# A planner that prefers matmuls whose operands have lain ready for a while

## The chip, the cores and the metric

The kernel runs on one core of one Trainium2 chip. The metric is the device time of one execution in microseconds (us); lower is better. Before the change the median of three runs is 1119.1 us (1116.96, 1119.1 and 1125.9).

## The reference

Attention over 4 batches, 8 heads, 768 positions and a head size of 64, in which a query sees only the keys whose 6 hash bits equal its own; its output goes through a two-layer feed-forward block with a squared ReLU.

```python
q_bits = (np.einsum('bhsd,dk->bhsk', q, proj) > 0).astype(np.int64)
k_bits = (np.einsum('bhsd,dk->bhsk', k, proj) > 0).astype(np.int64)
mask = q_bucket[:, :, :, None] == k_bucket[:, :, None, :]      # buckets: the 6 bits as a number
scores = np.where(mask, 0.125 * np.matmul(q, k.transpose(0, 1, 3, 2)), -1000000000.0)
attn = np.exp(scores - np.max(scores, axis=-1, keepdims=True))
attn = attn / (np.sum(attn, axis=-1, keepdims=True) + 1e-09)
x = np.matmul(attn, v)                       # then to [3072 tokens, 512]
r = np.maximum(x @ w_in, 0.0)                # w_in 512 x 2048
return (s * (r * r) + b) @ w_out             # w_out 2048 x 512
```

## The kernel before, in words

**Slots.** The attention is cut into 96 slots: one head of one batch and one chunk of 256 queries each. In batch 0 the 8 heads are visited once for chunk 0 and once for chunks 1 and 2; in batches 1 to 3 each head is visited once, for its three chunks. On TensorE (PE) a slot is a chain with steps of VectorE (DVE) between:

- scores: six matmuls with 256 columns (L527; L525 for the first eight slots) into banks 0 to 2 of PSUM; DVE takes the maximum (L532)
- two transposes of that maximum into bank 4 (L536); DVE reduces them (L538)
- one small transpose of the result into bank 4 (L540); DVE makes a row of it (L546)
- six matmuls that add this row and the low parts (L557); ScalarE (ACT) takes the exponential (L562)

These steps of PE are the slot's chain. What follows is not in it: the exponentials are split in two by ACT (L579) and GpSimd (POOL, L580) and go through the values matmuls (L586, L587) into bank 3; the sums of a row (L614) go to bank 4; and the operands of the head after next are prepared with transposes (L386), hash matmuls (L411 to L413) and a mean (L488), all in the other half of bank 4, which ACT and DVE read (L388, L389, L416).

**Feed-forward work.** The output of two heads goes to DRAM (`xd`), and when all 8 heads of a chunk are there it is loaded again (`xc`, four DMAs of 256 KB on SP's queue, L649). A chunk then takes 192 matmuls with 256 columns (L662, bank 5) and 96 with 512 columns (L679, banks 6 and 7). There are twelve chunks. The two tiles of `xc` hold one chunk, so the next chunk's load starts when the last L662 of the one before is done. Weights are made in batch 0 from decoded words.

**What sets the order.** Every step is recorded with an engine, a cost, the names that it reads and writes, and a priority `pr` (low goes first): chain and scores near 10 x the slot's number, the rest of the attention a little behind, feed-forward work at 1e5 and above. `Plan.order` plays the engines forward by these costs: a step's `ready` is the planned end of what it depends on plus a hop (`HOP`, 0.2 us behind PE, 0.06 behind DVE, ACT and POOL, 1.8 behind SP). When an engine is free, it takes among the steps that are ready the one with the lowest `(pr, index)`. So on PE the feed-forward matmuls fill whatever the attention leaves. The steps are then issued in the order of their planned starts, each engine works through its own list strictly in that order, and semaphores see to the real dependencies. The plan names the halves of bank 4 as two things, `("b", 4, 0)` for chain and sums and `("b", 4, 1)` for preparation.

```python
    def pe(cost, fn, r, w, pr):
        plan.add(PE, cost, fn, r, w, pr)
```

Of the kernel before, what the change touches and what calls it, by code (L numbers as in the profile page):

```python
# [31 lines left out]
class Plan:  # L32
# [3 lines left out]
    def __init__(self):  # L36
        self.steps = []
        self.writer = {}
        self.readers = {}

    def add(self, eng, cost, fn, r=(), w=(), pr=0.0, lag=0.0):
        i = len(self.steps)
# [15 lines left out]
    def order(self):  # L58
        n = len(self.steps)
        left = [len(s[5]) for s in self.steps]  # L60
        users = [[] for _ in range(n)]
        for i, s in enumerate(self.steps):
            for d in s[5]:
                users[d].append(i)
        ready = [0.0] * n
        free = {}
        moved = 0.0
        open_ = {}
        for i in range(n):
            if not left[i]:  # L70
                open_.setdefault(self.steps[i][0], []).append(i)
        out = []
        while len(out) < n:
            best = None
            for e, lst in open_.items():
                if lst:
                    t = max(free.get(e, 0.0), min(ready[i] for i in lst))
                    if best is None or t < best[0]:
                        best = (t, e)
            t, e = best  # L80
            rank = lambda i: (self.steps[i][3], i)
            i = min((i for i in open_[e] if ready[i] <= t), key=rank)
            i = min((j for j in open_[e] if ready[j] <= t + LOOK.get(e, 0.0) * self.steps[i][1] and rank(j) <= rank(i)), key=rank)
            open_[e].remove(i)
            eng, cost, fn, pr, lag, deps = self.steps[i]
            start = max(free.get(e, 0.0), ready[i])
            free[e] = start + cost
            end = start + cost + HOP[e]
            if e == SP:
                moved = max(moved, start + cost) + lag  # L90
                end += moved - start - cost
            else:
                end += lag
            out.append((start, i))
            for u in users[i]:
                ready[u] = max(ready[u], end - (SAME[e] if self.steps[u][0] == e else 0.0))
                left[u] -= 1
                if not left[u]:
                    open_.setdefault(self.steps[u][0], []).append(u)
        self.length = max(free.values())  # L100
        self.start = {i: t for t, i in out}
        return [i for _, i in sorted(out)]
# [2 lines left out]

HOP = {None: 0.0, PE: 0.2, DVE: 0.06, ACT: 0.06, POOL: 0.06, SP: 1.8}
SAME = {None: 0.0, PE: 0.2, DVE: 0.06, ACT: 0.06, POOL: 0.06, SP: 0.0}
LOOK = {DVE: 0.5, ACT: 0.0, POOL: 0.0}


@with_exitstack
def lsh_attention_moe(ctx: ExitStack, tc, q, k, v, proj, w_in, w_out, s, b, out):
    nc = tc.nc
# [32 lines left out]

        plan.add(SP, 0.7, lambda: nc.sync.dma_start(f32(dst()), f32(src())), r, w, pr, size / 2.6e5)

    def pe(cost, fn, r, w, pr):
        plan.add(PE, cost, fn, r, w, pr)  # L150

    def dve(n, fn, r, w, pr, ns=None):
        plan.add(DVE, ((n + 64) / 960.0 if ns is None else ns), fn, r, w, pr)
# [7 lines left out]
    def mmc(n, c):  # L161
        return c * (n / 2325.0 + 0.0095)
# [348 lines left out]
    def scores(i, pr):  # L511
# [7 lines left out]
        for p in range(NP_):  # L519
            def lead(p=p):  # L520
                for m in range(2):
                    o, kt = bank[:, pb[p], m * CH:(m + 1) * CH], slice((2 * p + m) * P, (2 * p + m + 1) * P)
                    if exact:
                        n = P if i < WARM else HR
                        nc.tensor.matmul(o, EK[h][0:n, kt], EQ[h][0:n, cs], start=m == 0, stop=m == 1, skip_group_check=True)  # L525
                        continue
                    nc.tensor.matmul(o, ks[0:HR + TPC, 0, kt], aq[0:HR + TPC, cs], start=m == 0, stop=m == 1, skip_group_check=True)  # L527
            pe(mmc(CH, 8 if exact else 2), lead, AK(x) + KK(x) if exact else AK(x, g=(c,))  + KK(x, (0, 2, 4)), [("b", pb[p])], pr)
        t, tk, nm, nk = MX, "mx", nmt[:, i % 4], ("nm", i % 4)

        sc = bank[:, b0:b0 + NP_].rearrange("p b (m n) -> p n b m", n=CH)
# [2 lines left out]
        def across():  # L534
            for j in range(TPC):
                nc.tensor.transpose(out=bank[:, 4, j * P:(j + 1) * P], in_=t[:, j * P:(j + 1) * P], identity=ident)  # L536
        pe(0.23, across, [tk], [("b", 4, 0)], pr)
        dve(CH, lambda: nc.vector.tensor_reduce(nm, bank[:, 4, 0:CH].rearrange("p (j n) -> p j n", j=TPC), AX.X, ALU.max, negate=True), [("b", 4, 0)], [nk], pr, 0.41)  # L538

        pe(0.115, lambda: nc.tensor.transpose(out=bank[0:TPC, 4, 0:P], in_=nm, identity=ident), [nk], [("b", 4, 0)], pr)  # L540
        mr, mk = (zhl[0:TPC, y], ("mrow", y)) if exact else (bq[0:TPC, cs], ("mr", x, c))

        def rows():
# [6 lines left out]
        for p in range(NP_):  # L550
            def rest(p=p):
                for m in range(2):
# [2 lines left out]
                        nc.tensor.matmul(o, oner[0:TPC], mr, start=False, stop=m == 1, skip_group_check=True)  # L555
                        continue
                    nc.tensor.matmul(o, ks[:, 1, kt], bq[:, cs], start=False, stop=m == 1, skip_group_check=True)  # L557
            pe(mmc(CH, 2), rest, [mk, tk] + ([] if exact else BK(x, g=(c,)) + KK(x, (1, 3))), [("b", pb[p])], pr)
        ES = [(npiece[0] + p) % (NE + 2 * NHL) for p in range(NP_)] if plain(i) else list(range(NP_))
        npiece[0] += NP_  # L560
        for p, z in enumerate(ES):
# [236 lines left out]
```

## Time and profile before

| what | value |
|---|---|
| median of three runs | 1119.1 us |
| the profiled execution's own time | 1128.45 us |
| its span | 1126.7 us |
| PE busy | 1063.8 us (94%), 6862 matmuls |
| weight loads of PE busy | 918.7 us (82%) |
| ACT, POOL, DVE busy | 700.5, 683.4, 655.9 us |
| mean granted clock of PE | 0.973 |

The span is what the profile sees of the execution; 1.75 us lie around it. PE is the engine with the most work by far. A matmul's end in this profile is modelled, so that idle time of PE shows only the part of a wait that reaches beyond it; the starts of consecutive matmuls and the idle time of the weight loads tell the rest.

### The profile page before, as it was taken

Reading aid. Unit: us, or ns where it says so; the run is one execution under the profiler, and the core shown is the slowest. Engines: PE = TensorE matmul, PEld = TensorE weight load, DVE = VectorE, ACT = ScalarE, POOL = GpSimd, SP = SyncE. Lnnn points to the kernel's source line nnn. Section 1 sums busy time; section 2 is a strip of 40 time slices with the busy share of each in tenths; the row PEclk is TensorE's granted clock in tenths of the full one; section 3 lists DMA queues with packets and bytes.
Section 4 is the critical chain, followed back from the end, with each engine's and each line's share of the span. In section 5 each row is a group of like instructions: output and inputs, shape, how many; then the busy total and the mean of one; then the engine's idle time right before and its main releaser. Section 6 shows DMA issues by size and latency. Waiting matters only on the chain.

```text
span 1126.7 us, 18822 instructions
## 1 busy us (share of the span) xinstructions
PE 1063.8 (94%) x6862; PEld 918.7 (82%) x6862; DVE 655.9 (58%) x807; ACT 700.5 (62%) x1377; POOL 683.4 (61%) x617
## 2 busy tenths in 40 slices
PE   8998788789999999999999999998999999999998
PEld 5665567678888888888888888887888998898987
DVE  5575767566676777677777677776776751000000
ACT  5566767566776777677766777776766773333332
POOL 4355788667576767676767676766676873222221
PEclk8888989899999999999999999999999999999999
DMA  7644444332422332332333243323232202101010
GB/s 164 177 134 133 121 139 138 91 83 72 117 72 62 109 93 74 87 99 57 81 99 89 59 111 77 80 62 118 55 79 82 64 11 75 38 19 56 1 57 19
DMA packets 99404, 94.49 MB, mean 84 GB/s; under 512 B 68528, under 2 KB 72112, under 8 KB 99312
## 3 DMA queue, kind: packets, MB, share of 16 engines
q1 hardware_dynamic: 94112, 76.24, 25.8%
q10 hardware_dynamic: 5200, 17.05, 5.0%
q8 instruction: 54, 0.88, 0.3%
q14 instruction: 38, 0.31, 0.1%
HBM read 49.81 MB, written 18.87 MB: 61 GB/s over the span
## 4 chain that ended last, share of the span: by engine, by line
PE 67%; DVE 4%; ACT 3%; issue 3%; POOL 3%; DMA 2%; SPq 0%; ACTq 0%; DVEq 0%; POOLq 0%
PE bank L662 21%; PE bank L679 20%; PE bank L557 5%; PE bank L527 4%; PE bank L587 4%; PE bank L586 4%; PE bank L536 2%; PE bank L614 2%; PE bank L386 2%; POOL hl L580 2%; DMA xd<-xsb 1%; PE bank L411 1%; PE bank L540 1%; ACT aq L388 1%; DVE nmt L538 1%
## 5 line engine op out<-in xcount | busy, mean ns | idle before, releaser
L580 POOL TENSOR_TENSOR hl<-et,hl 128x512 fp32r<-128x512 f32 x216 | 278.4, 1318 | 149.3 <-ACT hl L579 142.7
L662 PE MATMUL bank<-xc,w 128*128 128x256 f32 x2304 | 338.4, 286 | 6.8 <-DMA xc<-xd 5.7
L662 PEld LDWEIGHTS bank<-xc,w 128*128 128x128 f32 x2304 | 305.4, 189 | 17.1 <-DMA xc<-xd 3.4
L679 PE MATMUL bank<-w,ghb 128*128 128x512 f32 x768 | 257.7, 397 | 0.0
L670 POOL TENSOR_TENSOR glb<-rb,ghb 128x512 fp32r<-128x512 f32 x96 | 124.5, 1297 | 144.6 <-ACT ghb L669 134.1
L532 DVE TENSOR_REDUCE mx<-bank 128x256 f32<-128x1536 f32 x96 | 168.0, 1750 | 49.2 <-PE bank L527 30.2
L679 PE MATMUL bank<-w,glb 128*128 128x512 f32 x384 | 153.7, 403 | 0.0
L679 PEld LDWEIGHTS bank<-w,ghb 128*128 128x128 f32 x768 | 136.7, 188 | 16.9 <-issue 0.3
L608 DVE TENSOR_REDUCE zb<-et 128x256 f32<-128x1536 f32 x72 | 126.0, 1750 | 41.2 <-ACT et L562 38.6
L562 ACT ACTIVATE et<-bank 128x512 f32<-128x512 f32 x240 | 130.7, 621 | 26.1 <-PE bank L557 18.5
L667 ACT ACTIVATE rb<-bank 128x512 f32<-128x512 f32 x96 | 57.2, 595 | 142.6 <-PE bank L662 139.4
L579 ACT CAST hl<-et 128x512 fp32r<-128x512 f32 x216 | 128.6, 661 | 0.8
L527 PE MATMUL bank<-aq,ks 78*128 78x256 f32 x528 | 122.6, 316 | 2.1 <-ACT ex L562 1.5
L586 PE MATMUL bank<-hl,vs 128*128 128x256 f32 x432 | 119.7, 295 | 0.0
L587 PE MATMUL bank<-hl,vs 128*128 128x256 f32 x432 | 114.7, 286 | 1.1 <-POOL hl L580 0.8
L527 PEld LDWEIGHTS bank<-aq,ks 78*128 78x128 f32 x528 | 91.2, 197 | 14.9 <-ACT ex L562 3.7
L687 DVE SCALAR_TENSOR_TENSOR osb<-bank,misc,bcs 128x512 f32<-128x512 f32 x22 | 16.2, 745 | 140.8 <-PE bank L679 140.7
L618 ACT ACTIVATE xpb<-bank,vmn 64x256 f32<-64x256 f32 x96 | 45.0, 469 | 80.9 <-PE bank L587 80.0
L557 PE MATMUL bank<-bq,ks 128*128 128x256 f32 x528 | 82.3, 292 | 11.5 <-DVE bq L546 11.5
L587 PEld LDWEIGHTS bank<-hl,vs 128*128 128x128 f32 x432 | 81.9, 189 | 7.7 <-POOL hl L580 4.5
L624 DVE RECIPROCAL zpb<-zpb 128x256 f32<-128x256 f32 x48 | 83.7, 1744 | 3.2 <-ACT zpb L616 2.9
L557 PEld LDWEIGHTS bank<-bq,ks 128*128 128x128 f32 x528 | 70.5, 192 | 17.3 <-DVE bq L546 8.8
(111 smaller groups left out, 1676.6 us busy)
## 6 DMA issues: line engine op xcount, KB each, us to landing
xd<-xsb SPq DMA_DIRECT2D x48, 256.0 KB
xc<-xd SPq DMA_DIRECT2D x48, 256.0 KB
raw<-in_moe_w_in_dram ACTq DMA_DIRECT2D x16, 512.0 KB
raw<-in_moe_w_out_dram ACTq DMA_DIRECT2D x16, 512.0 KB
nat<-in_q_dram SPq DMA_DIRECT2D x32, 192.0 KB
nat<-in_k_dram SPq DMA_DIRECT2D x32, 192.0 KB
bq<-aq SPq DMA_DIRECT2D x32, 192.0 KB
out_dram<-osb SPq DMA_DIRECT2D x22, 256.0 KB
```

The lines of the kernel that those rows point to most:

```text
L527: nc.tensor.matmul(o, ks[0:HR + TPC, 0, kt], aq[0:HR + TPC, cs], start=m == 0, stop=m == 1, skip_group_check=True)
L532: dve(S * TPC, lambda: nc.vector.tensor_reduce(t, sc, AX.XY, ALU.max), [("b", b) for b in pb], [tk], pr, 1.75)
L557: nc.tensor.matmul(o, ks[:, 1, kt], bq[:, cs], start=False, stop=m == 1, skip_group_check=True)
L562: act(512, lambda p=p, z=z: nc.scalar.activation(et(z) if plain(i) else pairs(z), bank[:, pb[p]] if plain(i) else bank[:, pb[p]].rearrange ...
L579: act(512, lambda z=z, y=y: nc.scalar.copy(HL[2 * y].rearrange("p (m n) -> p m n", n=CH), pairs(z)), [("e", z)], [("hl", 2 * y)], pr)
L580: pool(512, lambda z=z, y=y: nc.gpsimd.tensor_tensor(HL[2 * y + 1].rearrange("p (m n) -> p m n", n=CH), pairs(z), f32(HL[2 * y]).rearrange ...
L586: nc.tensor.matmul(av, VS[w % 2][:, kt], HL[2 * y][:, ms], start=(kt == 0), stop=False)
L587: nc.tensor.matmul(av, VS[w % 2][:, kt], HL[2 * y + 1][:, ms], start=False, stop=(kt == NT - 1))
L608: dve(S * TPC, lambda: nc.vector.tensor_reduce(ZB, es, AX.XY, ALU.add), [("e", z) for z in range(NE)], ["zb"], pr, 1.75)
L662: nc.tensor.matmul(hp, wt[("wi", n, cc)][:, m % 2, fs], xc[:, m // 2, :], start=(cc == 0 and m == 0), stop=(cc == NC_ - 1 and m == 2))
L670: pool(2 * CH, lambda r=r, gh=gh, gl=gl: nc.gpsimd.tensor_tensor(gl, r, f32(gh), ALU.subtract), [rk, hk], [lk], MP)
L679: nc.tensor.matmul(bank[:, 6 + t, :], (gh, gh, gl)[n][:, ts], wt[("wo", f)][:, n % 2], start=(f == 0 and n == 0), stop=(f == NF - 1 and n ...
```

## The change

Each step of PE gets a margin: 0.4 us (`OFF`), or 0.05 us (`CHAIN`) for the steps of a slot's chain. The planner keeps, beside `ready`, the planned end (with hop) of the latest step of another engine that a step depends on (`other`). When PE is free it first looks at the ready steps whose `other` lies at least their margin back, and takes the one of the lowest rank among them; only if there is none it takes as before. Nothing is computed differently and the set of instructions is the same; only the order changes, on PE directly and on the other engines because the planned times that follow change.

```diff
+        self.soft = {}
...
-        ready = [0.0] * n
+        ready, other = [0.0] * n, [-9.0] * n
...
-            i = min((i for i in open_[e] if ready[i] <= t), key=rank)
-            i = min((j for j in open_[e] if ready[j] <= t + LOOK.get(e, 0.0) * self.steps[i][1] and rank(j) <= rank(i)), key=rank)
+            safe = [i for i in open_[e] if ready[i] <= t and other[i] + self.soft.get(i, CHAIN) <= t] if e == PE else []
+            i = min(safe, key=rank) if safe else min((i for i in open_[e] if ready[i] <= t), key=rank)
+            if not safe:
+                i = min((j for j in open_[e] if ready[j] <= t + LOOK.get(e, 0.0) * self.steps[i][1] and rank(j) <= rank(i)), key=rank)
...
                 ready[u] = max(ready[u], end - (SAME[e] if self.steps[u][0] == e else 0.0))
+                if self.steps[u][0] != e:
+                    other[u] = max(other[u], end)
...
+CHAIN = 0.05
+OFF = 0.4
...
-    def pe(cost, fn, r, w, pr):
+    def pe(cost, fn, r, w, pr, chain=False):
         plan.add(PE, cost, fn, r, w, pr)
+        if not chain:
+            plan.soft[len(plan.steps) - 1] = OFF
```

The calls for L525/L527, L536, L540 and L555/L557 pass `True`. Lines of the changed kernel stand up to 9 higher: what is L540 before is L549 there, L411 is L420, L557 is L566, L662 is L671, L679 is L688, L586 and L587 are L595 and L596.

**Place 1.** PE in slot 36 (batch 1), from the chain's small transpose to the matmuls behind it; `hl` and `vs` are values matmuls, `w`,`ghb`/`glb` and `xc`,`w` feed-forward, `pjh`/`pjl` the hash matmuls of a coming head. Before:

```order
L540 MATMUL bank<-ident,nmt 2x128
L679 MATMUL bank<-w_1434,ghb 128x512
L679 MATMUL bank<-w_1434,glb 128x512
L411 MATMUL bank<-aq_69,pjh 64x256
L412 MATMUL bank<-aq_69,pjl 64x256
L413 MATMUL bank<-bq_71,pjh 64x256
L557 MATMUL bank<-bq_70,ks_72 128x256 x6
```

The same place of the changed kernel:

```order
L549 MATMUL bank<-ident,nmt 2x128
L595 MATMUL bank<-hl_1894,vs_2505 128x256
L596 MATMUL bank<-hl_1901,vs_2505 128x256
L688 MATMUL bank<-w_1434,glb 128x512
L671 MATMUL bank<-xc_1_0_2177,w_1466 128x256 x2
L420 MATMUL bank<-aq_69,pjh 64x256
L421 MATMUL bank<-aq_69,pjl 64x256
L422 MATMUL bank<-bq_71,pjh 64x256
L566 MATMUL bank<-bq_70,ks_72 128x256 x6
```

Between the transpose and the hash matmuls stood two matmuls with 512 columns; now four with 256 and one with 512 stand there.

**Place 2.** PE in slot 41, from the small transpose to the six matmuls that use the row which DVE makes of it. Before:

```order
L540 MATMUL bank<-ident,nmt 2x128
L679 MATMUL bank<-w_676,glb 128x512
L679 MATMUL bank<-w_676,ghb 128x512 x2
L557 MATMUL bank<-bq_71,ks_73 128x256 x6
L614 MATMUL bank<-zhl,oner 128x256 x2
```

The same place of the changed kernel:

```order
L549 MATMUL bank<-ident,nmt 2x128
L671 MATMUL bank<-xc_2_0_3148,w_809 128x256
L671 MATMUL bank<-xc_2_1_3158,w_833 128x256 x3
L671 MATMUL bank<-xc_2_1_3158,w_857 128x256 x2
L497 MATMUL bank<-ones,vp 64x1
L566 MATMUL bank<-bq_71,ks_73 128x256 x6
```

Three matmuls with 512 columns are replaced by six with 256 and a mean.

**Place 3.** PE in slot 48, the first of batch 2, where the feed-forward work of batch 1's chunk 0 begins; the first matmul that reads the fourth load of that chunk is the one with `w_545`. Before:

```order
L540 MATMUL bank<-ident,nmt 2x128
L679 MATMUL bank<-w_1816,ghb 128x512 x2
L411 MATMUL bank<-aq_69,pjh 64x256
L412 MATMUL bank<-aq_69,pjl 64x256
L413 MATMUL bank<-bq_71,pjh 64x256
L557 MATMUL bank<-bq_70,ks_72 128x256 x6
L614 MATMUL bank<-zhl,oner 128x256 x2
L411 MATMUL bank<-aq_69,pjh 64x256
L412 MATMUL bank<-aq_69,pjl 64x256
L413 MATMUL bank<-bq_71,pjh 64x256
L527 MATMUL bank<-aq_68,ks_72 128x256 x2
L662 MATMUL bank<-xc_0_1_4146,w_545 128x256 x2
```

The same place of the changed kernel, where that matmul is the one with `w_547`:

```order
L595 MATMUL bank<-hl_1894,vs_3673 128x256
L596 MATMUL bank<-hl_1901,vs_3673 128x256
L549 MATMUL bank<-ident,nmt 2x128
L671 MATMUL bank<-xc_0_1_4105,w_547 128x256 x3
L671 MATMUL bank<-xc_0_0_4094,w_407 128x256 x3
L671 MATMUL bank<-xc_0_0_4094,w_421 128x256
L566 MATMUL bank<-bq_70,ks_72 128x256 x6
```

The first reader of the fourth load stood behind the slot's last matmuls and the next slot's first scores; now it stands straight behind the small transpose.

## Rows read from the trace of the kernel before

**Rows 1.** The view of stretches: busy us and instructions of each engine, clock, DMA.
```profile
core 0: us, PE busy (x) PEld busy (x) DVE busy (x) ACT busy (x) POOL busy (x), PEclk, DMA share, GB/s
...
100.00:250.00 150.00, 118.40 (x621) 96.18 (x621) 98.77 (x108) 96.92 (x186) 111.47 (x90) 0.90 0.43 121
250.00:930.00 680.00, 659.97 (x4576) 586.88 (x4575) 485.80 (x570) 481.61 (x976) 478.92 (x444) 1.00 0.31 79
930.00:1127.00 197.00, 191.96 (x1211) 172.40 (x1209) 9.93 (x14) 62.08 (x102) 46.66 (x39) 1.00 0.11 38
```

**Rows 2.** Waits of PE from 100 to 250 us: total, times, longest.
```profile
PE bank L557 <- DVE bq L546: 10.9, 8, 6.5
```

**Rows 3.** Groups by line from 250 to 930 us, PE: busy, mean, then idle before.
```profile
L662 PE MATMUL bank<-xc,w 128*128 128x256 f32 x1392 | 216.1, 286 | 4.0 <-DMA xc<-xd 3.9
...
L587 PE MATMUL bank<-hl,vs 128*128 128x256 f32 x430 | 114.2, 286 | 1.1 <-POOL hl L580 0.8
...
L614 PE MATMUL bank<-zhl,oner 128*128 128x256 f32 x142 | 30.8, 298 | 1.5 <-DVE bq L389 0.9
L536 PE MATMUL bank<-ident,mx 128*128 128x128 f32 x144 | 29.2, 284 | 2.7 <-DVE bq L389 1.0 <-ACT aq L388 0.6 <-DVE nat L416 0.2
L386 PE MATMUL bank<-ident,nat 128*128 128x128 f32 x134 | 26.7, 281 | 3.5 <-DVE nmt L538 1.7 <-DVE bq L546 0.9 <-DVE nat L416 0.4
L411 PE MATMUL bank<-aq,pjh 128*64 128x256 f32 x69 | 21.4, 310 | 2.0 <-DVE nat L416 0.4 <-DVE bq L546 0.4 <-DVE nmt L538 0.3
...
L540 PE MATMUL bank<-ident,nmt 128*2 128x128 f32 x72 | 19.5, 271 | 4.3 <-ACT aq L388 2.0 <-DVE nmt L538 1.3 <-DVE bq L389 0.5
```

**Rows 4.** The same view and stretch, weight loads (PEld).
```profile
L587 PEld LDWEIGHTS bank<-hl,vs 128*128 128x128 f32 x430 | 81.5, 189 | 7.7 <-POOL hl L580 4.5
...
L557 PEld LDWEIGHTS bank<-bq,ks 128*128 128x128 f32 x432 | 57.3, 191 | 4.2 <-DVE bq L546 3.3
...
L536 PEld LDWEIGHTS bank<-ident,mx 128*128 128x128 f32 x144 | 16.7, 140 | 10.9 <-ACT aq L388 4.1 <-DVE nat L416 1.7 <-DVE bq L389 1.6
L386 PEld LDWEIGHTS bank<-ident,nat 128*128 128x128 f32 x134 | 15.4, 140 | 9.3 <-DVE bq L546 4.6 <-DVE nmt L538 3.2 <-DVE nat L416 0.8
...
L411 PEld LDWEIGHTS bank<-aq,pjh 128*64 128x64 f32 x69 | 9.4, 136 | 10.3 <-DVE bq L546 4.4 <-DVE nmt L538 2.7 <-DVE bq L389 1.4
L540 PEld LDWEIGHTS bank<-ident,nmt 128*2 128x2 f32 x72 | 5.8, 81 | 10.3 <-DVE nmt L538 3.9 <-ACT aq L388 3.1 <-DVE bq L389 2.0
```

**Rows 5.** The timeline in slot 36: start, us, engine, line.
```profile
369.69 0.27 PE L540 MATMUL bank<-ident,nmt 128*2 128x128 f32 x1
...
370.00 0.41 DVE L546 SCALAR_TENSOR_TENSOR bq<-bank,ident 2x256 fp32r<-2x256 f32 x1 [0.36 <-PE bank L540]
...
370.46 0.13 PEld L411 LDWEIGHTS bank<-aq,pjh 128*64 128x64 f32 x1 [0.47 <-DVE bq L546]
```

**Rows 6.** The timeline of PE from 756 to 766 us.
```profile
756.60 1.36 PE L662 MATMUL bank<-xc,w 128*128 128x256 f32 x10
757.79 0.63 PE L679 MATMUL bank<-w,ghb 128*128 128x512 f32 x2
758.26 0.39 PE L679 MATMUL bank<-w,glb 128*128 128x512 f32 x1
...
765.31 0.62 PE L662 MATMUL bank<-xc,w 128*128 128x256 f32 x2 [2.83 <-DMA xc<-xd]
```

**Rows 7.** The view of stretches around that wait (columns as Rows 1).
```profile
765.00:770.00 5.00, 4.69 (x27) 4.72 (x28) 1.42 (x3) 1.67 (x4) 1.69 (x2) 0.66 0.02 9
```

**Rows 8.** The chain that ended last, at the first chunk of batch 1.
```profile
464.54 0.51 PE bank L614 x2
...
475.32 8.18 DMA xd<-xsb
483.52 2.60 DMA xc<-xd
486.16 0.50 PE bank L662 x2
```

More of the change, by code (lines that the diff above doesn't have):

```diff
@@ L527, in lead @@
                     nc.tensor.matmul(o, ks[0:HR + TPC, 0, kt], aq[0:HR + TPC, cs], start=m == 0, stop=m == 1, skip_group_check=True)
-            pe(mmc(CH, 8 if exact else 2), lead, AK(x) + KK(x) if exact else AK(x, g=(c,))  + KK(x, (0, 2, 4)), [("b", pb[p])], pr)
+            pe(mmc(CH, 8 if exact else 2), lead, AK(x) + KK(x) if exact else AK(x, g=(c,))  + KK(x, (0, 2, 4)), [("b", pb[p])], pr, True)
         t, tk, nm, nk = MX, "mx", nmt[:, i % 4], ("nm", i % 4)
@@ L536, in across @@
                 nc.tensor.transpose(out=bank[:, 4, j * P:(j + 1) * P], in_=t[:, j * P:(j + 1) * P], identity=ident)
-        pe(0.23, across, [tk], [("b", 4, 0)], pr)
+        pe(0.23, across, [tk], [("b", 4, 0)], pr, True)
         dve(CH, lambda: nc.vector.tensor_reduce(nm, bank[:, 4, 0:CH].rearrange("p (j n) -> p j n", j=TPC), AX.X, ALU.max, negate=True), [("b", 4, 0)], [nk], pr, 0.41)
-        pe(0.115, lambda: nc.tensor.transpose(out=bank[0:TPC, 4, 0:P], in_=nm, identity=ident), [nk], [("b", 4, 0)], pr)
+        pe(0.115, lambda: nc.tensor.transpose(out=bank[0:TPC, 4, 0:P], in_=nm, identity=ident), [nk], [("b", 4, 0)], pr, True)
         mr, mk = (zhl[0:TPC, y], ("mrow", y)) if exact else (bq[0:TPC, cs], ("mr", x, c))
@@ L557, in rest @@
                     nc.tensor.matmul(o, ks[:, 1, kt], bq[:, cs], start=False, stop=m == 1, skip_group_check=True)
-            pe(mmc(CH, 2), rest, [mk, tk] + ([] if exact else BK(x, g=(c,)) + KK(x, (1, 3))), [("b", pb[p])], pr)
+            pe(mmc(CH, 2), rest, [mk, tk] + ([] if exact else BK(x, g=(c,)) + KK(x, (1, 3))), [("b", pb[p])], pr, True)
         ES = [(npiece[0] + p) % (NE + 2 * NHL) for p in range(NP_)] if plain(i) else list(range(NP_))
```

## The prediction

> **What bounds the kernel now.** I read the stretches first [rows 1]. From 250 to 930 us PE is busy for 659.97 of 680 us at full clock, and behind the last attention slot, from 930 us on, for 191.96 of 197; no other engine passes 486 of the 680. So the time is PE's work plus PE's holes, and the order of PE's list can only change the holes. From 100 to 250 us there are holes of 31.6 us, the longest of them 6.5 us before L557 [rows 2]; there too little feed-forward work is decoded to fill them.
>
> The holes of the long stretch stand in the groups by line [rows 3]. 3.9 us are a wait for a load of `xc`. The others, L540 4.3, L386 3.5, L536 2.7, L411 2.0, L614 1.5 and L587 1.1 us, are short waits for DVE, ACT or POOL. A matmul's modelled end hides a part of such a wait, so these numbers are a lower bound. The weight loads stand idle longer at the same lines, 10.3, 9.3, 10.9 and 10.3 us at L540, L386, L536 and L411 [rows 4], which is an upper bound, since a load may also wait for its own turn.
>
> **Whom these waits are for.** L411 writes the upper half of bank 4, and the plan makes it depend on that half and on its operands alone. Yet in slot 36 it starts when L546 has ended, which reads the lower half [rows 5]: L540 starts at 369.69, L546 runs from 370.00 for 0.41 us, L411's weights come at 370.46 after 0.47 us idle. The same holds for L386 behind L538 and L546, and for L540, L536 and L614 behind L388, L389 or L416, which are the releasers that the two groups of rows name most [rows 3, 4]. So most short waits are between the halves of bank 4, and the plan does not know of them: a margin that is reckoned from planned dependencies cannot aim at them. Only L587 behind POOL's L580, and L557 and L540 behind their own DVE step, are waits that the plan knows.
>
> **The change part by part.** It adds and removes no instruction; planning is done before the chip runs.
>
> *Waits at bank 4.* I counted them in the two built orders. For slots 25 to 95 I took each PE instruction that waits for the DVE or ACT step behind an earlier group of PE, added up the PE work between that group and it, and compared this with the time that the step takes to answer. The work is priced by starts: 0.118 us for 256 columns, 0.23 for 512 (ten L662 start from 756.60 to 757.79, two L679 from there to 758.26 [rows 6]). The answer takes 0.72 us behind L540's end [rows 5], and as estimates from that row 0.75 to 0.8 us behind L386 or the hash matmuls, 1.3 us where both L388 and L389 have to be through. What is missing, summed, is:
>
> - L386, L411, L488 behind L538 or L546: 41 places short by 13.6 us before, 47 places by 3.2 us after. Place 1 shows why: an instruction that has its margin no longer follows two matmuls behind L540 but five, 0.46 us of work before and 0.70 after.
> - L536 and L614 behind L388, L389 or L416: 3.6 us before, 5.0 after.
> - L540 behind the same three: 2.5 us before, 0.7 after.
> - L557 and L540 behind their own DVE step: 0.9 us before, nothing after. This is the 0.05 us of the chain: of 71 slots, 49 had less than 0.8 us of work between L540 and L557, now 2 have (place 2: from 0.69 to 0.80).
>
> Together 20.7 us become 9.0: 57% of these waits go. So the margin helps where it was not aimed, by spreading what follows the chain. On the lower bound of the holes (14.0 us for the five lines without L587) this is 8 us, on the upper (40.8 for four of them) 23, on the count itself 11.7. I take 14, since the count leaves out that DVE is sometimes late by itself.
>
> *L587 behind POOL.* 0.8 us in the holes, 4.5 us in the weight loads [rows 3, 4], in short pieces that a margin of 0.4 us should cover: I take 2.5, bounds 0.8 and 4.5.
>
> *What the chain pays.* Where a step of the chain is passed over for a filler, the slot gets longer by that filler. PE works meanwhile, so this costs nothing as long as there is filler: at the last row sum of the attention 1,196 feed-forward matmuls are left before and 1,101 after, and the stretch behind it gets shorter by what the attention gets longer (some 14 us of work). Where there is no filler (slots 13, 14, 17 and 18, in the stretch from 100 to 250 us) the two orders are the same, since without a safe step the old choice stands: 0, bounds -4 and +4.
>
> *The first chunk of batch 1.* Here the cover is thin, and the change takes some of it. The path runs from slot 45's L614 at 464.54 over the normalization to the write of `xd` at 475.32, which needs 8.18 us, and the load of 2.60 us; the first reader starts at 486.16 [rows 8], after a wait of 1.1 us. By the same prices PE had 18.3 us of work between that L614 and the reader before; it has 15.1 after (place 3). The 3.2 us less become wait, if the path is no quicker. What a wait of such a size does to the clock shows at 762 us: after 2.83 us without a matmul [rows 6] the next 5 us ran at a mean granted clock of 0.66 [rows 7], so a good two thirds of them at 1.2 instead of 2.4 GHz, which gave 1.7 us less work. I take +5.
>
> *The other loads of `xc`.* Of the eight loads up to 930 us the one at 758 us was late because it stood behind a write of `xd` and four key copies on SP's queue; it cost 2.83 + 1.7 us. In the new order its neighbours are others, but two later loads have copies between their parts. I take 0, bounds -4.5 and +4.5.
>
> Sum: -14 - 2.5 + 5 = -11.5 us. The profiled execution took 1128.45 us, 9.35 above the median of 1119.1; the steps are the same in each, so I put the sum on the median: **1107.6 us** (a profiled execution like this one would take about 1117). About 1% is what runs of this kernel can tell from no change, since the three runs shown differ by 0.8%.
>
> **The rivals.**
>
> *The margin cannot see what is waited for.* If the waits between the halves stay as they are and only the planned ones go, L587's 2.5 us and about 3 at L557 and L540 are won (between the 0.9 us of the count and the 3.3 and 3.9 us that their weight loads name [rows 4]), and the batch boundary takes 5 back: about 1119. For it speaks that the releasers are mostly such steps; against it the count, 13.6 to 3.2. The Trainium skill's page "PSUM — Partial Sum Buffer", section "PSUM bank collisions raise a hardware error", says that PSUM has to be guarded by bank and quadrant of partitions and not by address, so that a wait between two halves of one bank cannot be wished away. The trace agrees on the wait, 0.47 us of idle weight loads at L411 [rows 5].
>
> *Slower: the loads of `xc` come late.* The change moves feed-forward work ahead of the attention, and with it each chunk's load into other traffic. Between a chunk's last L662 and the next chunk's first the new order has 4.5 to 6.4 us of PE work at the eight boundaries. At 758 us the same step took 7.5 us (the last L662 starts before 757.79, the next at 765.31 [rows 6]). If every load took that long, each boundary would wait 2.0 us more and lose 1.7 by the clock: 8 x 3.7 = 30 us, and with -16.5 and +5 the kernel would take about 1137; with six such loads about 1130, and from three on the gain is gone. Against it: two waits make up nearly all of the 3.9 us before, so six of the eight loads were there in time.
>
> *All of it goes.* The upper bounds, 23 and 4.5 us, with a path at the batch boundary that is as quick as it must be: 1119.1 - 27.5 = about 1092.
>
> **How the numbers follow.** Forecast, with a range of its own of 1100 to 1115: 0.50. Margin blind: 0.20. Loads late: 0.12, spread from 1122 to 1137. All of it: 0.18. Faster by over 1% (under 1107.9) is the last and a good half of the first: 0.45. Within 1% (to 1130.3): the rest of the first, the second, a part of the third: 0.45. Slower: 0.10. The range reaches from the last case to the lower half of the late loads: 1092 to 1125.
>
> **What would show it.** In the groups by line of the changed kernel the idle time before L386, L411 and L540 falls to about half, that of L587 and L557 to nearly nothing, that of L536 and L614 stays. At the first chunk of batch 1 there is a wait of 4 to 5 us for `xc`, with a dip of the clock behind it. The attention's last slot ends later, the stretch behind it is shorter. The first 250 us look alike. Wrong would be: holes that sum up as before (the margin is blind), or waits for `xc` at several boundaries.

## The result, and the profile after

The changed kernel takes 1109.74 us (median of four runs, 1107.84 to 1110.77), the kernel before, on the same chip, 1120.37: a ratio of 0.9899 with a 95% interval of 0.9854 to 0.9943. Measured again (e7 below) it is 0.9885 [0.9857, 0.9913]. The forecast was 1107.6 us and -11.5 us; measured are -10.6 us here and -13.0 in e7.

The profiled execution takes 1110.71 us, its span is 1108.9. Line numbers are 9 higher than before. The view of stretches of the changed kernel, as in [rows 1]:

```profile
core 0: us, PE busy (x) PEld busy (x) DVE busy (x) ACT busy (x) POOL busy (x), PEclk, DMA share, GB/s
100.00:250.00 150.00, 122.47 (x647) 100.27 (x648) 98.55 (x112) 99.85 (x194) 117.48 (x96) 0.92 0.43 121
250.00:930.00 680.00, 661.92 (x4663) 599.97 (x4663) 484.73 (x571) 480.62 (x978) 477.70 (x443) 1.00 0.31 81
930.00:1109.00 179.00, 173.11 (x1095) 156.40 (x1093) 6.75 (x11) 56.46 (x92) 41.35 (x33) 1.00 0.09 32
```

From 250 to 930 us PE starts 4663 matmuls instead of 4576, in the same time and at the same clock, although its busy time rose by 2 us only. So most of what was won had not been visible as idle time of PE. The weight loads show it: they are busy for 13 us more. The groups by line of the weight loads, 250 to 930 us, answer to [rows 4]; the idle time stands behind the second bar:

```profile
L596 PEld LDWEIGHTS bank<-hl,vs 128*128 128x128 f32 x432 | 82.1, 190 | 7.0 <-POOL hl L589 2.8
...
L566 PEld LDWEIGHTS bank<-bq,ks 128*128 128x128 f32 x432 | 57.4, 189 | 4.7 <-DVE bq L555 3.0
...
L623 PEld LDWEIGHTS bank<-zhl,oner 128*128 128x128 f32 x144 | 22.2, 188 | 3.5 <-DVE nat L425 1.4 <-DVE bq L398 0.9 <-issue 0.2
L545 PEld LDWEIGHTS bank<-ident,mx 128*128 128x128 f32 x142 | 15.9, 141 | 17.9 <-DVE nat L425 6.8 <-DVE bq L398 3.9 <-ACT aq L397 3.8
L395 PEld LDWEIGHTS bank<-ident,nat 128*128 128x128 f32 x132 | 15.6, 141 | 2.0 <-DVE nmt L547 0.7 <-DVE bq L555 0.2
...
L420 PEld LDWEIGHTS bank<-aq,pjh 128*64 128x64 f32 x69 | 9.3, 134 | 2.2 <-DVE nmt L547 0.5 <-ACT zpb L625 0.2
...
L549 PEld LDWEIGHTS bank<-ident,nmt 128*2 128x2 f32 x72 | 5.9, 81 | 7.3 <-DVE bq L398 5.1 <-DVE nat L425 0.9 <-DVE nmt L547 0.4
```

L395 and L420, the preparation, fell from 9.3 and 10.3 us to 2.0 and 2.2. L549, the small transpose, fell from 10.3 to 7.3. But L545, the first transposes of the chain, rose from 10.9 to 17.9, and 14.5 us of that end with a reader of the other half of bank 4 (L397, L398, L425). L623, the row sums, fell to 3.5 us from this line of before:

```profile
L614 PEld LDWEIGHTS bank<-zhl,oner 128*128 128x128 f32 x142 | 21.9, 191 | 5.3 <-DVE bq L389 3.1 <-ACT et L562 0.7 <-issue 0.6
```

PE's groups by line in the same stretch say the same with smaller numbers, beside [rows 3]:

```profile
L671 PE MATMUL bank<-xc,w 128*128 128x256 f32 x1464 | 228.9, 287 | 5.1 <-DMA xc<-xd 4.9
...
L596 PE MATMUL bank<-hl,vs 128*128 128x256 f32 x432 | 113.4, 283 | 2.1 <-POOL hl L589 2.0
...
L545 PE MATMUL bank<-ident,mx 128*128 128x128 f32 x142 | 29.6, 290 | 6.0 <-ACT aq L397 2.2 <-DVE nat L425 1.9 <-DVE bq L398 1.4
L395 PE MATMUL bank<-ident,nat 128*128 128x128 f32 x132 | 25.8, 276 | 0.3 <-DVE nmt L547 0.3
L420 PE MATMUL bank<-aq,pjh 128*64 128x256 f32 x69 | 20.2, 293 | 0.0
L549 PE MATMUL bank<-ident,nmt 128*2 128x128 f32 x72 | 19.5, 271 | 2.7 <-DVE bq L398 1.9 <-DVE nat L425 0.7
```

**Three stretches and one sum.** For every run I counted the first matmuls of the scores in its trace, six to a slot (twelve in the first eight slots), and so cut the profiled span at the starts of slots 25 and 49. Slots 25 to 48 are those in which the feed-forward work of batch 0 runs out and batch 1's begins. "Bank 4" is the idle time of the weight loads at the six lines that write it (before: L386, L411, L488, L536, L540, L614) and at L412, 250 to 930 us; "all" is that of all lines. "Filler" is how many feed-forward matmuls stand ahead of slot 48. Batch 0 supplies 3 chunks of 288, and nine more can start with the first three loads of the next chunk: 873.

```
run                    0-25   25-49  49-end  span    bank 4  all    filler
before                258.9   225.7   642.0  1126.7   50.8   93.3   842
e1 before again       252.5   225.7   641.5  1119.6   49.7   91.5   842
after                 253.7   222.4   632.8  1108.9   36.3   80.0   860
e7 after again        250.5   222.4   631.8  1104.7   36.4   80.2   860
e2 chain only         248.4   238.4   650.5  1137.3   61.0  110.8   873
e3 margin only        255.4   231.9   634.9  1122.3   40.7   88.8   867
e4 margin 0.8         256.7   228.3   631.5  1116.5   47.7   86.1   867
e8 margin 0.45        254.0   225.5   627.7  1107.3   33.9   76.4   865
e6 loads planned late 261.5   226.5   641.7  1129.6   45.6   90.5   873
e5 bank planned       243.8   246.6   623.3  1113.8   32.9   87.7   873
e9 window only        255.3   220.9   641.5  1117.7   40.2   84.5   800
e10 margins, window   239.4   229.5   626.4  1095.3   39.2   80.8   873
e11 window early      236.2   228.1   635.0  1099.3   37.1   85.5   873
e12 early, 0.45       246.6   226.4   628.6  1101.6   38.1   79.8   873
```

From before to after the two stretches behind slot 25 lose 12.5 us, and all idle time of the weight loads 13.3, of which 14.5 at bank 4. A single profile of each kernel does not separate the first stretch from chance: with the same order it took 258.9 us and 252.5.

Two things help to read the table. Ahead of slot 49 nearly the same feed-forward work is done, 865 matmuls before and 873 to 885 in the others (830 in e9). Ahead of slot 25 it is not: 181 to 189 in eight runs, 218 to 245 in e2, e5, e6, e10, e11 and e12, so for these the first two stretches are best taken together (up to slot 49 e10 takes 468.9 us and e11 464.3, after 476.1). And the time behind slot 25 goes with "all" and not with "bank 4" alone: e3 has 9 to 10 us less at bank 4 than the kernel before and takes as long (866.8 us), e4 has 2 to 3 us less and is 7 to 8 us quicker (859.8).

### The profile page after: what moved, and what is told of

It reads as the page before. It is cut to its first block, busy times and chain, and to the rows that moved or that the text cites. A ratio compares the mean times of both kernels' runs of the same rounds, so it can differ in the third digit from the quotient of the medians.

```text
span 1108.9 us, 18843 instructions
## 1 busy us (share of the span) xinstructions
PE 1051.0 (95%) x6862; PEld 918.6 (83%) x6862; DVE 651.9 (59%) x807; ACT 696.9 (63%) x1377; POOL 683.0 (62%) x617
## 4 chain that ended last, share of the span: by engine, by line
PE 70%; DVE 6%; issue 2%; ACT 2%; DMA 1%; POOL 0%; SPq 0%; DVEq 0%; ACTq 0%; POOLq 0%
PE bank L671 22%; PE bank L688 20%; PE bank L566 5%; PE bank L536 5%; PE bank L596 4%; PE bank L595 4%; PE bank L545 2%; DVE mx L541 2%; PE bank L623 2%; DMA xc<-xd 1%; PE bank L395 1%; PE bank L593 1%; PE bank L549 1%; DVE nat L425 1%; DVE zb L617 1%
## 5 line engine op out<-in xcount | busy, mean ns | idle before, releaser
L671 PE MATMUL bank<-xc,w 128*128 128x256 f32 x2304 | 341.7, 287 | 9.2 <-DMA xc<-xd 6.7
L671 PEld LDWEIGHTS bank<-xc,w 128*128 128x128 f32 x2304 | 305.2, 190 | 17.6 <-DMA xc<-xd 8.0
L688 PE MATMUL bank<-w,ghb 128*128 128x512 f32 x768 | 256.2, 398 | 0.0
L679 POOL TENSOR_TENSOR glb<-rb,ghb 128x512 fp32r<-128x512 f32 x96 | 124.2, 1294 | 137.9 <-ACT ghb L678 129.4
L688 PE MATMUL bank<-w,glb 128*128 128x512 f32 x384 | 153.7, 402 | 0.0
L688 PEld LDWEIGHTS bank<-w,ghb 128*128 128x128 f32 x768 | 136.3, 189 | 16.1 <-issue 0.5
L536 PE MATMUL bank<-aq,ks 78*128 78x256 f32 x528 | 120.6, 313 | 2.9 <-ACT ex L571 2.1
L595 PE MATMUL bank<-hl,vs 128*128 128x256 f32 x432 | 116.2, 289 | 0.3 <-ACT hl L588 0.3
L596 PE MATMUL bank<-hl,vs 128*128 128x256 f32 x432 | 113.4, 283 | 2.1 <-POOL hl L589 2.0
L536 PEld LDWEIGHTS bank<-aq,ks 78*128 78x128 f32 x528 | 91.7, 197 | 15.6 <-ACT ex L571 4.3
L696 DVE SCALAR_TENSOR_TENSOR osb<-bank,misc,bcs 128x512 f32<-128x512 f32 x22 | 16.2, 746 | 127.3 <-PE bank L688 127.2
L566 PE MATMUL bank<-bq,ks 128*128 128x256 f32 x528 | 80.4, 288 | 10.2 <-DVE bq L555 9.9
L596 PEld LDWEIGHTS bank<-hl,vs 128*128 128x128 f32 x432 | 82.1, 190 | 7.0 <-POOL hl L589 2.8
L595 PEld LDWEIGHTS bank<-hl,vs 128*128 128x128 f32 x432 | 82.1, 190 | 3.8 <-ACT hl L588 0.7
L566 PEld LDWEIGHTS bank<-bq,ks 128*128 128x128 f32 x528 | 70.6, 190 | 16.8 <-DVE bq L555 9.7
```

The source lines that it names most:

```text
L595: nc.tensor.matmul(av, VS[w % 2][:, kt], HL[2 * y][:, ms], start=(kt == 0), stop=False)
L596: nc.tensor.matmul(av, VS[w % 2][:, kt], HL[2 * y + 1][:, ms], start=False, stop=(kt == NT - 1))
L671: nc.tensor.matmul(hp, wt[("wi", n, cc)][:, m % 2, fs], xc[:, m // 2, :], start=(cc == 0 and m == 0), stop=(cc == NC_ - 1 and m == 2))
L679: pool(2 * CH, lambda r=r, gh=gh, gl=gl: nc.gpsimd.tensor_tensor(gl, r, f32(gh), ALU.subtract), [rk, hk], [lk], MP)
L688: nc.tensor.matmul(bank[:, 6 + t, :], (gh, gh, gl)[n][:, ts], wt[("wo", f)][:, n % 2], start=(f == 0 and n == 0), stop=(f == NF - 1 and n ...
```

## Experiments

Ratios are to the kernel before, measured on the same chip in the same round, with 95% intervals. Edits are against the changed kernel.

**e1 and e7, the kernel before and the changed one once more.** No edit.

> The kernel before, unchanged, for a second profile. If the 5 us that the changed kernel's profile gained ahead of slot 25 (258.9 to 253.7 us) belong to the order, this profile reaches slot 25 at 259 us again, within 1 us; if they are the difference of one execution from another, it reaches it anywhere from 253 to 259. In slots 25 to 95 the starts should repeat: 36 us of short waits, of which 11.6 are of preparation steps behind L538 or L546.

> The changed kernel, unchanged, for a second profile and a tighter ratio. From slot 25 to the end the kernel before took 867.8 and 867.1 us in two executions, the changed one 855.2 in one. If the gain belongs to the order of slots 25 to 95, this one takes 854 to 857 us for that, with the same short waits within 1 us, whatever the first 250 us do; ratio 0.987 to 0.992. If the first profile was a lucky execution: over 860.

e1: 1121.44 us. e7: 1109.43, 0.9885 [0.9857, 0.9913]. In both, slots 25 to 48 take what they took before and after, and the rest does to within 1 us, but the first 25 slots are 6.4 and 3.2 us shorter. So the profiled execution behind the prediction was long in its first 250 us by chance (252.5 us lie even a little below the expected 253 to 259), and what follows can be compared to within 1 us.

**e2 and e3, each margin alone.**

e2:

```diff
-OFF = 0.4
+OFF = 0.0
```

e3:

```diff
-CHAIN = 0.05
+CHAIN = 0.0
```

> The margin of the chain's steps alone (0.05 us), no margin for the others. If the gain comes from the spread of the other steps (the theory of the prediction), this wins at most the 2 to 3 us of the chain's own waits: ratio 0.997 to 1.0, and the waits of preparation steps behind L538 or L546 stay at 10 to 13 us. If the chain's own margin makes the gain: ratio 0.990. If any new order is worth a per cent by chance, anything from 0.985 to 1.01.

> The margin of the steps outside the chain alone (0.4 us), none for the chain. If the spread of these steps makes the gain: ratio 0.988 to 0.993, with the waits of preparation steps behind L538 or L546 at 1 to 4 us as in the changed kernel. In its built order only 4 preparation steps stand with 0.02 to 0.7 us of work behind L536 or L540 (43 before, 17 in the changed kernel) and 11 chain steps or row sums 0.1 to 0.8 us behind a preparation step (37 and 28), so by that count it should even be a little better than the changed kernel, 0.985 to 0.99. If the chain's margin makes the gain: 0.998 to 1.002.

e2: 1142.62 us, 1.0168 [1.0119, 1.0217]. e3: 1123.54, 0.9998 [0.9970, 1.0026]. The weight loads of e2, 250 to 930 us:

```profile
L566 PEld LDWEIGHTS bank<-bq,ks 128*128 128x128 f32 x420 | 57.6, 195 | 2.5 <-DVE bq L555 1.0
...
L395 PEld LDWEIGHTS bank<-ident,nat 128*128 128x128 f32 x132 | 14.9, 141 | 9.5 <-DVE nmt L547 3.5 <-DVE bq L555 2.8 <-DVE nat L425 1.4
...
L420 PEld LDWEIGHTS bank<-aq,pjh 128*64 128x64 f32 x67 | 9.2, 137 | 11.3 <-DVE bq L555 4.4 <-DVE nmt L547 3.8 <-ACT zpb L625 1.3
L549 PEld LDWEIGHTS bank<-ident,nmt 128*2 128x2 f32 x70 | 5.7, 81 | 13.3 <-DVE nat L425 4.5 <-ACT aq L397 4.3 <-DVE bq L398 3.5
```

And those of e3:

```profile
L566 PEld LDWEIGHTS bank<-bq,ks 128*128 128x128 f32 x432 | 57.5, 193 | 10.2 <-DVE bq L555 9.6
...
L395 PEld LDWEIGHTS bank<-ident,nat 128*128 128x128 f32 x134 | 16.5, 142 | 0.6 <-ACT vmn L463 0.4
L545 PEld LDWEIGHTS bank<-ident,mx 128*128 128x128 f32 x144 | 15.8, 140 | 16.3 <-DVE bq L398 8.4 <-ACT aq L397 3.1 <-DVE nat L425 3.1
...
L420 PEld LDWEIGHTS bank<-aq,pjh 128*64 128x64 f32 x69 | 9.3, 134 | 0.9
L549 PEld LDWEIGHTS bank<-ident,nmt 128*2 128x2 f32 x72 | 5.8, 81 | 15.7 <-DVE bq L398 9.9 <-DVE nat L425 4.5 <-DVE nmt L547 0.6
```

The margin of 0.4 us alone takes the preparation's waits away (1.5 us at L395 and L420 instead of 19.6 [rows 4]), and the chain's margin alone does not (20.8). But with the first alone the chain pays: its own last step L566 stands idle for 10.2 us, 9.6 of them behind the DVE step that the plan knows, and L549 for 15.7. So beside the larger margin the 0.05 us keeps one wait from turning into another. By itself it is harmful. That its order runs out of filler (873 ahead of slot 48) is the smaller part of this: of the 16 us that slots 25 to 48 take more than after, 3.3 lie in slot 48, and why the slots ahead of it are longer stays open. Both runs missed what was expected of them: neither margin alone wins time, and the two together do.

**e4 and e8, the size of the margin.** `OFF = 0.8` and `OFF = 0.45`.

> The margin outside the chain doubled to 0.8 us. If the margin works by covering errors of the plan, a longer one covers more: ratio 0.983 to 0.989, L587 behind POOL under 1 us. If the gain is in where the preparation steps happen to fall against the chain, which the plan does not know, there is no order in it: by the count of the built order (30 steps short behind the chain instead of 17) it should be a little worse than the changed kernel, 0.990 to 0.996.

> The margin outside the chain at 0.45 instead of 0.4 us, nothing else. If the margin as such makes the gain, a neighbour of 0.4 does the same: ratio 0.987 to 0.993. By the count of its built order it should be as good or better (6.4 us short at bank 4 against 9.0, the same 1,101 feed-forward matmuls behind the last row sum). If the changed kernel's per cent is the luck of one order among many, the ratio is anywhere from 0.985 to 1.005.

e4: 1114.97 us, 0.9938 [0.9914, 0.9963]. e8: 1107.96, 0.9865 [0.9835, 0.9895]. At 0.8 the loads at L545 stand idle for 23.8 us, and bank 4 gives back most of its gain (47.7); most of what e4 still wins stands at other lines. At 0.45 bank 4 stands at 33.9. A neighbouring value does as well as 0.4 and a larger one worse. This suggests that the size acts through the sequence at bank 4 that the plan happens to build, not as a wait that grows shorter; no run shows it by itself.

**e5, the plan is told of bank 4.** A step that writes bank 4 counts as having lain ready only if every reader of the bank that is already placed was through its margin ago.

```diff
+        if any(k[:2] == ("b", 4) for k in (*r, *w)):
+            self.four.add(i)
...
-            safe = [i for i in open_[e] if ready[i] <= t and other[i] + self.soft.get(i, CHAIN) <= t] if e == PE else []
+            safe = [i for i in open_[e] if ready[i] <= t and max(other[i], four if i in self.four else -9.0) + self.soft.get(i, CHAIN) <= t] if e == PE else []
...
+            if e != PE and i in self.four:
+                four = max(four, end)
```

> The margins of the changed kernel, and the planner told of the waits between the halves: a PE step that touches bank 4 counts as safe only when every step of ACT or DVE on bank 4 that has been planned so far ended its margin ago. If the waits between the halves are what is left (20 of 32 us of short waits in slots 25 to 95), most of them go: under 8 us of such waits and a ratio to the kernel before of 0.975 to 0.985. The price is a longer slot: 921 feed-forward matmuls are left behind the last row sum instead of 1,101, which costs nothing as long as PE has them as filler. If instead the longer slots starve the filler at the batch boundaries or the waits are of another kind, it is no better than the changed kernel: 0.988 to 1.0.

1115.57 us, 0.9923 [0.9897, 0.9949]: slower than the change as it is. Its parts differ, though. Slots 25 to 48 take 246.6 us, 24 more than after, and the rest 623.3, 9.5 less. Of the 24 us, 13 lie in slots 25 to 41, where PE does 612 feed-forward matmuls instead of 500 at full clock: that is work done earlier. The other 11 lie in slots 42 to 48 (75.1 us instead of 64.2). These are shown by the stretches of the feed-forward's first layer in e5, where there is nothing for 40 us, and the second layer's line has nothing either (busy us and count of that line, then the clock of PE, the share of DMA and GB/s):

```profile
440.00:450.00 10.00, 0.00 (x0) 0.57 0.39 120
450.00:460.00 10.00, 0.00 (x0) 0.75 0.31 79
460.00:470.00 10.00, 0.00 (x0) 0.94 0.31 68
470.00:480.00 10.00, 0.00 (x0) 0.84 0.35 73
```

This order puts more feed-forward work into the slots: the 873 matmuls are used up in slot 43, and even ahead of slot 46 the changed kernel has placed only 803. From there the attention runs without cover until batch 1's first load. Behind that, from 490 us on, the weight loads of e5 at L536, L386 and L411 of before show what the plan had been missing:

```profile
L551 PEld LDWEIGHTS bank<-ident,mx 128*128 128x128 f32 x88 | 11.2, 140 | 3.4 <-DVE bq L404 1.4
L401 PEld LDWEIGHTS bank<-ident,nat 128*128 128x128 f32 x84 | 10.3, 140 | 1.2 <-DVE bq L561 1.1
L426 PEld LDWEIGHTS bank<-aq,pjh 128*64 128x64 f32 x43 | 6.1, 141 | 0.2
```

The changed kernel's L545 stands idle for 10.0 us from its slot 49 on (476 to 930 us), mostly with the releasers of the other half. All of bank 4 together stands idle for 12.5 us in e5 from slot 49 to the last row sum, and for 22.1 us after; the difference is about the 9.5 us by which the rest is shorter. Of all the runs, this one ties the waits at bank 4 to the time most closely.

**e6, loads of `xc` planned 3 us later for their readers.**

```diff
-                end += moved - start - cost
+                end += moved - start - cost + self.late.get(i, 0.0)
...
+XCLATE = 3.0
...
+                plan.late[len(plan.steps) - 1] = XCLATE
```

> The changed kernel with the planned landing of the loads of xc put 3 us later, for their readers alone. The changed kernel waits 6.7 us for these loads, 3.4 us of it once, with the clock behind it at half. If these waits cost what they show, they fall to 2 us or less and the kernel gains 4 to 7 us on the changed one: ratio to the kernel before 0.983 to 0.987. If the later readers only move the hole (too little filler between two chunks), it stays at 0.988 to 0.993.

1126.37 us, 1.0027 [1.0009, 1.0044]. The waits for these loads do go (0.6 us of idle PE at their readers from 250 to 930 us instead of 5.1), yet the gain of the whole change is lost. The order falls differently: at bank 4 the loads of the chain's first transposes (L545 after) are idle for 22.8 us instead of 17.9 and the sum is 45.6 instead of 36.3, those of the values matmuls for 16.0 us instead of 10.8, and the filler is used up ahead of slot 48. Which of these costs most was not separated; the profile is of e6's slowest execution (1131.44 us). The wait of 5 us that went was worth less than the new order cost.

**e9 and e10, no preparation just ahead of the chain.** A step outside the chain that writes bank 4 is put off, as long as PE has another step to take, until the placed readers are through and no chain step of the bank becomes ready within 1.3 us; e9 without the two margins (both 0), e10 with them.

```diff
+            if any(i in self.four and i in self.soft for i in safe):
+                soon = any(j in self.four and j not in self.soft and t - 0.2 < ready[j] <= t + AHEAD for j in open_[e])
+                safe = [i for i in safe if i not in self.four or i not in self.soft or four <= t and not soon]
...
+AHEAD = 1.3
```

> No margins at all (both 0), but steps of bank 4 outside the chain are put off while a planned step of ACT or DVE on bank 4 is under way, or a chain step on bank 4 becomes ready within 1.3 us. If the waits between the halves are what the order can win, they fall from 25 us in slots 25 to 95 to under 8, with the slots as short as before (1,216 feed-forward matmuls left behind the last row sum): ratio 0.980 to 0.988. If the gain of the changed kernel came from the margin at other steps (values behind POOL, the chain's own), this wins nothing of it: 0.995 to 1.005.

> The changed kernel's margins and the rule that keeps bank 4's other steps out of the chain's way together. If both add up: ratio 0.975 to 0.985. The feed-forward work of batch 0 is used up at slot 48 in its built order (873 of the 873 that do not need batch 1's last heads), one slot earlier than in the changed kernel; if running out of filler costs more than the waits, as in the kernel that counted all of bank 4 for the chain too, it is 0.99 to 1.0.

e9: 1116.64 us, 0.9957 [0.9937, 0.9977]. e10: 1096.52, 0.9778 [0.9742, 0.9815], the quickest of all and 1.1% under the changed kernel. The rule alone removes waits too (bank 4 at 40.2, all at 84.5), but is worth less than half of the change; the margins are worth more beside it. In e10 the surprise is the first stretch: 239.4 us, 11 to 14 less than in the changed kernel's two profiles, with 35 feed-forward matmuls more done in it; from slot 25 on all three take 854 to 856.

**e11 and e12, the rule in the early slots alone.** The rule only for steps with a priority under 250 (slots 0 to 24); e12 with `OFF = 0.45` as well.

```diff
-            if any(i in self.four and i in self.soft for i in safe):
+            if any(i in self.four and i in self.soft and self.steps[i][3] < EARLY for i in safe):
```

> The margins of the change, with the window rule only for the steps of PE whose priority lies under 250, that is for the slots 0 to 24; later slots choose as in the changed kernel. The output is the reference's. Theory: what the window rule gave on top of the change comes from the head preparations of slots 4 to 9, which stand elsewhere then, and not from the waits at bank 4 that the rule was made for. Then slot 25 begins at about 240 us instead of 250 to 254, the rest from there takes the 855 us of the changed kernel, and the ratio to the kernel before is 0.975 to 0.982. Rival: the late slots carry the gain, and the early difference of the one profile was a variation of that execution: slot 25 begins at 250 us or later, ratio 0.985 to 0.992.

> As the run before, with a margin of 0.45 us in place of 0.4 for all steps outside the chain. The output is the reference's. Theory: the two gains add, since they lie in different slots: the early rule's 10 to 12 us before slot 25 and the 1 to 2 us that the margin of 0.45 gave behind it; ratio 0.972 to 0.981, the quickest version. Rival: with another margin the early slots fall into another order, and the early gain is a matter of that one order: ratio 0.983 to 0.990.

e11: 1103.57 us, 0.9836 [0.9809, 0.9863], between the two expectations. In its profile (1101.05 us, the quickest of its six executions) slot 25 begins at 236.2 us, so the early gain is real and belongs to the early order. But the rest takes 863.1 instead of 855: an order that reaches slot 25 earlier has used more filler (218 feed-forward matmuls by then instead of 183) and is short of it at slot 48. The stretches of e11 show both, a clock of 0.96 early and 91.20 busy us at a clock of 0.93 around the batch boundary:

```profile
30.00:110.00 80.00, 74.47 (x394) 50.52 (x392) 61.12 (x75) 55.81 (x110) 43.81 (x38) 0.96 0.48 147
400.00:500.00 100.00, 91.20 (x602) 81.86 (x601) 67.22 (x82) 65.25 (x134) 65.59 (x62) 0.93 0.31 81
```

The changed kernel in the same stretches:

```profile
30.00:110.00 80.00, 74.40 (x353) 49.45 (x352) 49.91 (x67) 48.92 (x98) 40.20 (x35) 0.86 0.54 153
400.00:500.00 100.00, 96.63 (x682) 87.49 (x681) 73.84 (x86) 73.13 (x149) 72.24 (x68) 1.00 0.30 81
```

e10 pays the same at the boundary (229.5 us) and gets it back behind slot 49 (626.4 against 635.0 of e11). There its gain is not at bank 4, whose loads stand idle for 22.4 us in e10 and 22.2 in e11, although the rule was made for them; less idle are the loads of the values matmuls (4.7 us against 8.4) and of the feed-forward's first layer (10.2 against 12.8). So e10 has an early and a late gain, and that the late one comes from the waits between the halves is not shown. e12 took 1106.3 us, 0.9863 [0.9836, 0.9890], no better than e8: the two gains do not add. With another margin the early slots fall into another order (slot 25 at 246.6 us, in an execution at the lower end of e12's 1103.4 to 1109.12).

## Why the prediction was right, and where not

**Waits at bank 4, -14: right in size, the count behind it not.** The weight loads name -14.5 us from 250 to 930 us, e1 and e7 -13.3. That a margin which cannot know these waits still removes most of the preparation's was the point of the count (13.6 to 3.2 us), and e3 shows that the 0.4 us does it. PE's own holes, the lower bound, would not have told: at L540, L386, L536 and L411 they went from 12.5 us to 9.0. The shares were off: L386 and L411 gave 15.4 us, L540 3.0 of its 10.3 instead of half, and L536 with L614 took back 5.2 (16.2 to 21.4) where the count had 1.4.

The step that failed is the time that the readers of the preparation take to answer, 0.75 to 1.3 us by the prediction's estimates from a single DVE step. (Its 0.72 us, too, holds from L540's start and not from its end [rows 5].) In the trace of before, from slot 25 on, L388 is through 1.3 us after the last L386 starts and L389 4.3 us after it, each the median. Slot 36 is one case, in which DVE has longer steps to do first:

```profile
362.54 0.38 PE L386 MATMUL bank<-ident,nat 128*128 128x128 f32 x2
...
366.23 0.48 ACT L388 ACTIVATE aq<-bank,misc 128x256 fp32r<-128x256 f32 x1
...
369.17 0.47 DVE L389 SCALAR_TENSOR_TENSOR bq<-bank,misc,aq 128x256 fp32r<-128x256 f32 x1
...
369.69 0.08 PEld L540 LDWEIGHTS bank<-ident,nmt 128*2 128x2 f32 x1 [0.17 <-DVE bq L389]
```

In the built orders the places where a chain or sum step follows a preparation with under 0.1 us of work between are 12 before and 37 after, and each of them is exposed to so late a reader. For e3 the count promised even more than for the change, yet the loads at L545 and L549 stood idle for 32.0 us there, most of it behind L398 (L389 before). So that the count came near the sum is in part luck. The rival of the blind margin is half right: the margin moved a part of these waits from the preparation to the chain. The Trainium skill's rule that the prediction named (page "PSUM — Partial Sum Buffer", section "PSUM bank collisions raise a hardware error") agrees with the trace: of 17.9 us of idle loads at L545, 14.5 stand behind readers of the other half.

**The chain's own waits, within these 14 us: half right.** L540's loads stood idle behind their own step L538 for 3.9 us before [rows 4] and for 0.4 after. L557's behind L546 stayed, 3.3 us before and 3.0 after (4.2 and 4.7 in all). Alone, the 0.05 us does shorten that wait (1.0 us in e2); beside the 0.4 us, which alone makes it 9.6 (e3), it only holds it where it was.

**L587 behind POOL, -2.5: not borne out.** The part of the loads' idle time that ends with POOL fell from 4.5 to 2.8 us, but the whole only from 7.7 to 7.0, and the idle time of PE rose from 1.1 to 2.1, nearly all of it two waits of 1.0 us. The margin did not cover these two.

**What the chain pays, nothing: right while there is filler.** The last row sum starts at 928.0 us instead of 931.9; reckoned from the start of slot 25 that is 1.3 us later (674.3 against 673.0), and the stretch behind it is 13.9 us shorter (some 14 forecast). Where filler runs out there is a price: six orders that have used up all 873 ahead of slot 48 (e2, e5, e6, e10, e11 and e12) take 4 to 24 us more in slots 25 to 48 than the changed kernel. These figures are not clean prices, since they hold other losses too (e2) and work that was moved from one stretch to another (e5); and e3, which has 6 of them left there, loses 9.5 us. I had asked for this cover only up to slot 18 and over the load of batch 1; the supply of 873 is the tighter bound, and the change left 13 of it ahead of slot 48.

**The first chunk of batch 1, +5: wrong, nothing came.** I held the path's 8.18 and 2.60 us [rows 8] fixed and took away the work over it. SyncE's queue in e1, with the order of before:

```profile
463.95 1.26 SPq L147 DMA_DIRECT2D ks<-aq  x2
466.37 1.27 SPq L649 DMA_DIRECT2D xc<-xd  x3
468.13 0.62 SPq L147 DMA_DIRECT2D ks<-aq  x1
468.85 0.37 SPq L147 DMA_DIRECT2D xd<-xsb  x1
469.31 1.50 SPq L147 DMA_DIRECT2D ks<-bq  x1
476.66 0.32 SPq L649 DMA_DIRECT2D xc<-xd  x1
```

The same queue in the changed kernel:

```profile
461.17 1.11 SPq L658 DMA_DIRECT2D xc<-xd  x2
466.69 0.32 SPq L154 DMA_DIRECT2D xd<-xsb  x1
468.71 0.32 SPq L658 DMA_DIRECT2D xc<-xd  x1
472.24 2.00 SPq L154 DMA_DIRECT2D ks<-aq  x3
```

The write of `xd` was long where three loads and three key copies were issued just ahead of it. In the new order the copies come later and the loads earlier, the load follows the write after 2.0 us instead of 7.8 (8.2 in the first profile of before, 2.0 again in e7), and the first reader at 473.90 us waits for nothing. That the company on the queue is the cause fits all four profiles, but no run changed it alone. Slots 25 to 48 became 3.3 us shorter. So the step that failed is the fixed path: the work over it did shrink, and the path shrank more.

**The other loads, 0 +- 4.5: right.** The wait moved. At 738 us a load that was issued behind four key copies made PE wait 3.4 us, and the clock around it fell as at 758 us before [rows 6, 7]. From the timeline of the changed kernel:

```profile
727.32 1.93 SPq L154 DMA_DIRECT2D ks<-aq  x3
...
729.68 0.78 SPq L154 DMA_DIRECT2D ks<-bq  x1
...
730.58 2.88 SPq L658 DMA_DIRECT2D xc<-xd  x2
...
738.86 1.44 PE L671 MATMUL bank<-xc,w 128*128 128x256 f32 x5 [3.38 <-DMA xc<-xd]
```

And the stretches around it:

```profile
735.00:740.00 5.00, 1.62 (x10) 1.42 (x9) 1.58 (x2) 0.65 (x2) 4.93 (x5) 0.83 0.28 91
740.00:745.00 5.00, 5.00 (x38) 4.96 (x38) 2.05 (x4) 1.08 (x3) 0.00 (x0) 0.82 0.14 32
```

**The early slots, 0: right.** 253.7 and 250.5 us against 258.9 and 252.5. L566 behind its DVE step waits 9.7 us in eight pieces from 100 to 250 us, as before 10.9 [rows 2].

So -11.5 came out as -12.5 behind slot 25, with two errors that partly cancel: the +5 did not come, nor did most of the -2.5. That the sum is so near is in part luck.

**What stays open.** Why the clock of 30 to 110 us is 0.97 in e10 and 0.86 after, with the same busy time of PE, was not taken apart. And a plan that knows bank 4 as e5 does, but keeps filler for slots 46 to 48, was not tried; its parts (222.4 us and 623.3) give an estimate of some 9 us less than the changed kernel behind slot 25. And how much of the gain belongs to the margins as such and how much to this one order cannot be told: the five orders that have both margins and no window rule lie between 0.9865 (e8) and 1.0027 (e6).

## What to carry to other kernels

A planner's margin can help where its model lacks a dependency, but blindly: of the 18.4 us that it took from three lines at bank 4 (L386, L411, L540) it gave 5.2 back at two others, and each new value is a new order. A count in the built order is as good as its answer times: take them from the trace for every reader, since an engine that is busy elsewhere answers late. Filler is a stock: count how much of it is left where the next supply begins, since an order that is quicker earlier may pay a part of it back there. Where PE looks 97% busy, read the idle time of the weight loads and the number of matmuls in a stretch, and cut the span at fixed points of the work before you compare two runs.

## What had not been expected of the hardware

The same order took 258.9 and 252.5 us up to slot 25, and from there 867.7 and 867.2. A write of 256 KB to DRAM was followed by the load that depends on it after 2.0 us where nothing was issued just ahead, and after 7.8 us behind three loads and three copies. From 30 to 110 us PE was busy for 74.4 us in one order and 74.5 in another, and did 353 and 397 matmuls, at mean granted clocks of 0.86 and 0.97 (the clock has two levels, 1.2 and 2.4 GHz).
